# Memory numerators and denominators in one 136-column matmul per block, with the head gate folded into the memory matrix and new bias values for the scheduler

## The chip, the cores and the metric

The kernel runs on one core of a Trainium2 chip. The metric is the device time of one execution in microseconds. A run that is read closely comes with a profile of one execution. The profile's own span is about 1.7 us shorter than the time of the same run (268.6 us in the profile against 270.2 us timed, for the kernel before), so I compare spans with spans and times with times.

The engines are called PE (TensorE matmul), PEld (its weight loads), DVE (VectorE), ACT (ScalarE), POOL (GpSimd) and SP (SyncE, which issues most loads here). "PE idle" means that neither a matmul nor a weight load starts. One more number: the granted clock of PE. Most executions show 1.0, some 0.994 or less. For one core the program names as slow only runs more than 1.5% above the fastest of the same kernel, so runs with a clock of 0.994 may be labelled fast.

## The reference, cut to what matters

```python
# x: 2048 tokens, 512 wide; 32 heads of 16; 4 segments of 512 tokens
for s in range(4):
    qs, ks, vs = q[s], k[s], v[s]
    a_dot = softmax(qs @ ks.T * 0.25 + causal_mask) @ vs       # attention in the segment
    pq    = phi(qs)                                            # t>0: t+1, else exp(t)
    num   = pq @ M                                             # per head: 16 x 16 memory
    den   = pq @ z + 1e-6                                      # per head: 16-vector
    o     = g * num / den + (1 - g) * a_dot                    # g = sigmoid(beta), per head
    M    += phi(ks).T @ vs ;  z += phi(ks).sum(0)
a = concat(o) @ wo
b = (gelu(x @ w_gate) * (x @ w_up)) @ w_down                   # feed-forward, 512 -> 1792 -> 512
out = G * a + (1 - G) * b                                      # G = sigmoid(x . gate_w), per token
```

Segment 0 has no memory yet, so the memory part (num, den) runs three times, for segments 1, 2 and 3. The kernel computes it while PE works on the attention of the segment before.

## The kernel before: the parts that the argument touches

The program is a graph of tasks. A list scheduler places the tasks on the engines at build time, using estimated durations and a priority for each task. The priority is the longest estimated path below the task plus a bias value by the task's name. The result is one fixed order of instructions per engine. Loads are tasks of SP in the same graph.

```python
class Task:
    def __init__(self, name, alts, grp=None, after=(), bias=0.0, nbytes=0):
        self.bias = bias + BIAS.get(name[:re.search(r"[_.]|$", name).start()], 0.0)
...
        for t in reversed(topo):
            best = max([s.prio for s in t.succs] + [0.0])
            t.prio = min(t.est.values()) + best + t.bias
```

Attention of one row of heads: PE fills four score banks (`qk`), ACT takes the exp of all four at once (2048 columns), POOL masks, PE multiplies by the values (`pv`). There is only one set of score banks, so a fill waits for the exp of the fill before. In the gaps PE works on projections and the feed-forward, which rotate through four other banks (`psW`).

```python
prev_exp[0] = exp_task(s, f"exp{s}_{t}{name}", [Instr(lambda e: e.activation(
    dst[:], XALL[:, :].rearrange("p (g c) -> p g c", g=4), ACTF.Exp, scale=ATT_SCALE),
    [("X", g) for g in range(4)], [key], act_t(2048))], after=after)
```

The memory part, once per segment: 16 matmuls of 8 columns for the denominators, one DVE chain over them, then four groups of four matmuls of 128 columns for the numerators, each group evicted by one DVE multiply.

```python
pieces(f"den{s}", gd, [mm(gd, lambda qt=qt, t=t: gd.f32()[:, 32 * qt + 8 * t:32 * qt + 8 * t + 8],
                          phq[:, t, qt * 128:(qt + 1) * 128], MZbd[:, t, 16:136:17],
                          [("phq", t), ("MZbd", t)], True, True, 8)
                       for qt in range(4) for t in range(4)], 16)
task(f"denp{s}", DVE, [ ... add EPS, reciprocal (128 columns), multiply by Gm = G/(1-G) * g ... ])
for qt in range(4):
    pieces(f"num{s}_{qt}", gn, [mm(... 128 columns of MZbd[:, t, :] ...) for t in range(4)], 4)
    task(f"nump{s}_{qt}", DVE, [ ... otok = numerators * ndsc ... ], grp=gn)
```

The softmax here doesn't subtract the row's maximum and nothing guards it: scores larger than these inputs give would overflow.

Of the kernel before, what the change touches and what calls it, by code (L numbers as in the profile page):

```python
# [7 lines left out]
PE, ACT, DVE, POOL, SP = "pe", "act", "dve", "pool", "sp"  # L8
ENGINES = (PE, ACT, DVE, POOL, SP)

BF = mybir.dt.bfloat16
F32 = mybir.dt.float32
# [4 lines left out]
H = 32  # L17
# [18 lines left out]
    "D0": -106, "D1": -371, "D2": -43, "G0": -115, "G1": -247, "G2": -35, "G3": -378, "GdT0": 15, "GdT1": -60,  # L36
    "GdT2": 3, "GdT3": 30, "Gev0": 33, "K0": 3, "K1": -10, "K2": -10, "K3": -1, "Q0": 511, "Q1": -156, "Q2":
    -52, "Q3": -9, "U0": -34, "U1": 29, "U2": -14, "U3": -56, "Um0": 79, "Um1": 211, "Um2": 371, "V0": -1,
    "V2": 35, "Vev0": -104, "Vev1": 13, "Vev2": -60, "Vev3": -8, "Vlo0": -17, "Vlo2": -45, "den1": -2, "den2":
    -79, "den3": -12, "denp1": 8, "denp2": 6, "denp3": -190, "exp0": -301, "exp1": 30, "exp2": 6, "exp3":  # L40
    -129, "exsT0": 21, "exsT1": -14, "exsT2": 18, "exsT3": 15, "fin1": 4, "fin2": -31, "fin3": 65, "gate1":
    -309, "gate2": 79, "gate3": 2, "gelu0": 59, "gelu1": 464, "gelu2": -99, "gelu3": 47, "gexs0": -8, "gexs1":
    89, "gexs2": -293, "gexs3": 30, "gts0": -81, "gts1": -16, "gts2": 38, "gts3": -58, "kl0": -6, "kl1": 87,
    "kl2": 6, "kl3": -10, "kp0": -27, "kp1": 26, "kp2": 4, "kp3": 7, "msk1": -15, "msk2": 6, "msk3": 331,
    "mz0": 13, "mz1": 73, "mz2": 71, "mzacc0": -41, "mzacc1": -32, "mzacc2": -48, "mzbd0": -4, "mzbd2": 15,
    "norm1": -39, "norm2": 27, "norm3": -67, "num1": -760, "num2": -501, "num3": -80, "nump1": 383, "nump2":
    100, "nump3": 303, "oTd1": -9, "oTd2": -167, "oTd3": 66, "omg": 37, "pkT0": 62, "pkT2": 20, "pkc0": -46,
    "pkc2": -100, "pke0": 8, "pke2": 96, "pqc1": 89, "pqc2": -47, "pqc3": 27, "pqe1": 414, "pqe2": 41, "pqe3":
    1, "pv0": 210, "pv1": -139, "pv2": 95, "pv3": 98, "pvt0": 307, "pvt1": -156, "pvt2": 59, "pvt3": -4,
    "qk0": 13, "qk1": -19, "qk2": 49, "qk3": -61, "x2": 45, "x3": 76  # L50
# [301 lines left out]
def dve_t(n, mode=1, psum=False, ap=False):  # L352
    return max(0.19, 0.155 + n / mode / 960.0 + (0.06 if ap else 0.0))
# [11 lines left out]
def _build(es, nc, A_x, A_wq, A_wk, A_wv, A_wo, A_beta, B_w_gate, B_w_up, B_w_down, gate_w, out):  # L365
    def sb(name, shape, dtype=BF):
        return es.enter_context(nc.sbuf_tensor(name, shape, dtype))
# [24 lines left out]
    bdmask = sb("bdmask", [P, 2, 17])  # L392
    gatew = sb("gatew", [P, 4])
# [5 lines left out]
    exs = sb("exs", [P, 16], F32)  # L399
    stmp = sb("stmp", [P, 16], F32)  # L400
# [4 lines left out]
    Gm = [sb(f"gm{i}", [P, 4, H], F32) for i in range(2)]  # L405
    ndsc = sb("ndsc", [P, 4, H], F32)
# [28 lines left out]
    def task(name, eng, instrs, **kw):  # L435
        return S.add(Task(name, {eng: instrs}, **kw))
# [5 lines left out]
    def pieces(name, g, instrs, size, after=(), bias=0.0):  # L442

        r = None
        for i in range(0, len(instrs), size):
            r = task(f"{name}.{i}", PE, instrs[i:i + size], grp=g, after=after, bias=bias)
        return r
# [36 lines left out]
    def xdma(s, after=()):  # L484
        for kb in range(4):
# [10 lines left out]
    warm = PT[R_PT - 1][:, 0, :]  # L496
    wkey = ("PT", R_PT - 1)
# [5 lines left out]
    task("warm0", DVE, [Instr(lambda e: e.memset(warm[:, 0:128], 0.0), writes=[wkey], est=0.15)], bias=9999.0)  # L503
    task("tload", ACT, [Instr(lambda e: e.activation(stmp[:, 0:1], warm[:, 0:1], ACTF.Exp), reads=[wkey],
                              writes=[("stmp",)], est=1.5)], bias=8000.0)
# [15 lines left out]
    for i in range(7):  # L521
        gw = Grp(banks)
        n = 4 if i < 6 else 2
        task(f"warm{i}", PE, [Instr(lambda e, gw=gw, n=n: e.matmul(  # L524
            gw.f32()[:, 0:128 * n].rearrange("p (o c) -> p o c", c=128), warm[:, 0:128],
            warm[:, 0:128].rearrange("p (o c) -> p o c", o=1).to_broadcast([P, n, 128]), start=True, stop=True),
            [wkey], [gw.key], 0.107 * n)], grp=gw, bias=5000.0 - i)
# [50 lines left out]
    def gate_head():  # L578
        exp_task(0, "gexp", [Instr(lambda e: e.activation(gexp[:], betab[:], ACTF.Exp), [("w", "beta")],
                                   [("c", "gexp")], 0.25)])  # L580
        task("gmat", DVE, [
            Instr(lambda e: e.tensor_scalar(gtmp[:], gexp[:], 1.0, None, ALU.add), [("c", "gexp")],
                  [("c", "gtmp")], 0.2),
            Instr(lambda e: e.reciprocal(gtmp[:], gtmp[:]), [("c", "gtmp")], [("c", "gtmp")], 0.25),
            Instr(lambda e: e.tensor_tensor(gmat[:], gexp[:], gtmp[:], ALU.mult), [("c", "gexp"), ("c", "gtmp")],
                  [("c", "gmat")], 0.2)])
        omg = task("omg", POOL, [Instr(lambda e, g=g: e.tensor_copy(
            omgT[32 * g:32 * g + 32, :].rearrange("p (t j) -> p t j", j=2),
            gtmp[32 * g:32 * g + 32, :].rearrange("p (t g j) -> p g t j", g=4, j=2)[:, g]),
            [("c", "gtmp")], [("c", "omgT", g)], 0.3) for g in range(4)])  # L590
        for ins in omg.alts[POOL]:
            ins.fence = True
# [48 lines left out]
    def prep(s):  # L641
# [29 lines left out]
        for j in range(2):  # L671
# [10 lines left out]
        bc = lambda a: a.rearrange("p (a o) -> p a o", o=1).to_broadcast([P, 4, H])  # L682
        bh = lambda a: a.rearrange("p (o h) -> p o h", o=1).to_broadcast([P, 4, H])
# [4 lines left out]
            + ([Instr(lambda e: e.tensor_tensor(Gm[sl][:], bc(exs[:, s4]), bh(gmat[:]), ALU.mult),  # L688
                      [("exs", s), ("c", "gmat")], [("Gm", sl)], 0.3)] if s > 0 else []))
# [10 lines left out]
        if s > 0:  # L700
            for i in range(2):
                phi_task("pq", s, ph, qT[sl], ("qT", sl), phq, "phq", i)
            gd = Grp(banks)
            pieces(f"den{s}", gd, [mm(gd, lambda qt=qt, t=t: gd.f32()[:, 32 * qt + 8 * t:32 * qt + 8 * t + 8],
                                      phq[:, t, qt * 128:(qt + 1) * 128], MZbd[:, t, 16:136:17],
                                      [("phq", t), ("MZbd", t)], True, True, 8)
                                   for qt in range(4) for t in range(4)], 16)
            nf = ndsc[:].rearrange("p a h -> p (a h)")
            task(f"denp{s}", DVE, [
                Instr(lambda e: e.tensor_scalar(nf, gd.f32()[:, 0:128], EPS, None, ALU.add), [gd.key], [("nd",)],  # L710
                      0.3),
                Instr(lambda e: e.reciprocal(nf, nf), [("nd",)], [("nd",)], 0.95),
                Instr(lambda e: e.tensor_tensor(ndsc[:], ndsc[:], Gm[sl][:], ALU.mult), [("nd",), ("Gm", sl)],
                      [("nd",)], 0.3)], grp=gd)
            for qt in range(4):
                gn = Grp(banks)
                pieces(f"num{s}_{qt}", gn, [
                    mm(gn, lambda gn=gn, t=t: gn.f32()[:, 128 * t:128 * t + 128].rearrange("p (h e) -> p h e", e=16),
                       phq[:, t, qt * 128:(qt + 1) * 128],
                       MZbd[:, t, :].rearrange("p (h c) -> p h c", c=17)[:, :, 0:16],  # L720
                       [("phq", t), ("MZbd", t)], True, True, 128) for t in range(4)], 4)
                task(f"nump{s}_{qt}", DVE, [
                    Instr(lambda e, gn=gn, qt=qt: e.tensor_tensor(
                        otok[:, qt % 2, :].rearrange("p (h e) -> p h e", e=16),
                        gn.f32()[:, :].rearrange("p (h e) -> p h e", e=16),
                        ndsc[:, qt, :].rearrange("p (h o) -> p h o", o=1).to_broadcast([P, H, 16]), ALU.mult),
                        [gn.key, ("nd",)], [("otok", qt % 2)], dve_t(512))], grp=gn)
                dma(f"oTd{s}_{qt}", SP, lambda qt=qt: oT[sl][:, :, qt * 128:(qt + 1) * 128],
                    lambda qt=qt: otok[:, qt % 2, :], [("otok", qt % 2)], [("oT", sl, qt, t) for t in range(4)], 262144,
                    issue=1.25, transpose=True)  # L730

    def memory(s):
        sl = s % 2
        if s < NSEG - 1:
# [18 lines left out]
            else:  # L753
# [6 lines left out]
                bdmask[32 * c:32 * c + 32].rearrange("p (o j) e -> p o (j e)", o=1).to_broadcast([32, 4, 34]),  # L760
                ALU.mult), [("MZacc",)] + [("c", "bd", j) for j in range(2)], [("MZbd", t) for t in range(4)], 0.3)
# [339 lines left out]
```

## Time and profile before

| | before |
|---|---|
| time | 270.2 us (270.0 to 270.5, 4 runs) |
| span in the profile | 268.6 us |
| PE / ACT / DVE / POOL busy | 97% / 79% / 69% / 35% |
| first projection starts | 5.51 us |
| start-to-start steps of the 96 memory matmuls, as recorded | 3.70 + 1.83 us |

A start-to-start step is the time from the start of one matmul to the start of the next one on PE. I work with these because busy times of pipelined matmuls overlap and can't be added.

The page of the kernel before: busy time with share and instruction count, then the chain of work that ended last, by engine and by line.

```profile
PE 259.8 (97%) x3075; PEld 122.3 (46%) x3118; DVE 185.8 (69%) x333; ACT 211.9 (79%) x179; POOL 95.2 (35%) x223
...
PE 95%; issue 2%; ACT 2%; DVE 0%; ACTq 0%
```

The list of waits of the same kernel (us in total, times, longest):

```profile
ACT pt L782 <- PE psXALL L775: 24.3, 44, 1.0
PEld psXALL L775 <- ACT pt L782: 22.9, 54, 0.4
...
PE psW L524 <- DVE pt L503: 1.1, 1, 1.1
```

In the list of waits the matmul row of PE waits only at the warm-up. But for the weight loads of the score fills the list names ACT's exp in 54 of 72 fills. The length of these waits says nothing: the weight loads stand 0.42 us before all 69 fills that have such a wait, and in 10 of the 54 the exp had ended more than 0.2 us earlier. The line only points at the right place. The timeline decides: of the 68 fills that follow an exp of the same stretch, 50 start within 0.2 us of its end (0.055 us at the least), and 18 come 0.28 to 1.2 us after it. So PE comes to most fills just when the exp ends. In turn ACT waits for the fill. The two form a loop, and PE's other work has been cut to its length.

The groups of the memory part before (line, engine, operation, tiles, shapes, count, then busy us, mean ns of one, and idle time before them):

```profile
L723 DVE TENSOR_TENSOR otok<-psW,ndsc 128x512 bf16<-128x512 f32 x12 | 7.8, 681 | 7.9 <-PE psW L439 7.9
...
L439 PE MATMUL psW<-mzbd,phq 128*128 128x128 bf16 x48 | 4.2, 223 | 0.0
...
L712 DVE RECIPROCAL ndsc<-ndsc 128x128 f32<-128x128 f32 x3 | 2.9, 952 | 0.1
...
L439 PE MATMUL psW<-mzbd,phq 128*128 128x8 bf16 x48 | 1.7, 176 | 0.0
```

Finally one turn of the loop in the timeline of the kernel before, with the 16 denominator matmuls in it (start us, duration us, then as above):

```profile
46.53 0.41 PE L775 MATMUL psXALL<-qT,klow 32*128 32x64 bf16 x32
...
47.13 1.88 ACT L782 ACTIVATE ptl<-psXALL 128x2048 bf16<-128x2048 f32 x1 [0.16 <-PE psXALL L775]
...
47.32 0.58 PE L439 MATMUL psW<-mzbd,phq 128*128 128x8 bf16 x16
...
47.96 1.24 PE L439 MATMUL psW<-xT,wk 128*128 128x512 bf16 x5
...
49.13 0.12 PEld L775 LDWEIGHTS psXALL<-qT,kpad 32*128 32x128 bf16 x8 [0.42 <-ACT ptl L782]
...
49.73 1.88 ACT L782 ACTIVATE pt<-psXALL 128x2048 bf16<-128x2048 f32 x1 [0.23 <-PE psXALL L775]
```

### The profile page before, as it was taken

How to read it: one execution, taken by the hardware profiler on the slowest of the kernel's cores; microseconds unless marked ns; L12 is line 12 of the kernel's file. 1: busy time of each engine (PE TensorE's matmuls, PEld its weight loads, DVE VectorE, ACT ScalarE, POOL GpSimd, SP SyncE). 2: the span in 40 equal slices, each digit the busy share in tenths (PEclk: the TensorE clock that was granted, in tenths of full speed). 3: DMA queues.
4: the chain of work that ended last, by engine and by line, in shares of the span. 5: the costliest groups of instructions: out<-in, count | busy, mean ns of one | idle time of the engine just before them, and what ended most of it. 6: DMA issues, size and time to landing. Idle time of an engine off the chain costs nothing.

```text
span 268.6 us, 7243 instructions
## 1 busy us (share of the span) xinstructions
PE 259.8 (97%) x3075; PEld 122.3 (46%) x3118; DVE 185.8 (69%) x333; ACT 211.9 (79%) x179; POOL 95.2 (35%) x223
## 2 busy tenths in 40 slices
PE   8999999999999999999999999999999999999996
PEld 5445344444445444544444444444354434444354
DVE  1678997988978659798525988798851677353451
ACT  3889987999998898889768898877777767677602
POOL 8328853542002843252201574252300252352300
PEclk9999999999999999999999999999999999999999
DMA  6998991000304510102011310213020000000002
GB/s 194 203 323 185 362 212 22 4 0 2 81 2 98 81 42 0 45 20 42 20 24 39 60 23 1 58 27 82 1 44 0 2 0 2 20 22 32 9 2 78
DMA packets 32056, 16.53 MB, mean 62 GB/s; under 512 B 21400, under 2 KB 32024, under 8 KB 32024
## 3 DMA queue, kind: packets, MB, share of 16 engines
q1 hardware_dynamic: 31736, 15.81, 25.4%
q8 instruction: 24, 0.39, 0.6%
q10 hardware_dynamic: 288, 0.26, 0.3%
q14 instruction: 8, 0.07, 0.1%
HBM read 8.14 MB, written 2.10 MB: 38 GB/s over the span
## 4 chain that ended last, share of the span: by engine, by line
PE 95%; issue 2%; ACT 2%; DVE 0%; ACTq 0%
PE psW L439 75%; PE psXALL L775 9%; PE psW L824 6%; PE psXALL L439 1%; PE psW L832 1%; PE psW L524 1%; PE psW L742 1%; ACT pt L782 1%; PE psXALL L533 1%; ACT hT L909 1%; ACT L909 0%; ACT ost L958 0%; DVE pt L503 0%; ACTq L336 0%
## 5 line engine op out<-in xcount | busy, mean ns | idle before, releaser
L782 ACT ACTIVATE pt<-psXALL 128x2048 bf16<-128x2048 f32 x64 | 120.0, 1875 | 27.4 <-PE psXALL L775 24.3
L786 POOL TENSOR_SCALAR_AFFINE_SELECT pt<-pt 128x256 bf16<-128x256 bf16 x128 | 55.4, 434 | 139.3 <-ACT pt L782 132.7
L439 PE MATMUL psW<-xT,wu 128*128 128x512 bf16 x214 | 51.0, 379 | 1.1 <-issue 0.8
L439 PE MATMUL psW<-xT,wg 128*128 128x512 bf16 x213 | 50.3, 380 | 1.4 <-issue 1.1
L439 PE MATMUL psW<-wd,hT 128*128 128x512 bf16 x201 | 49.9, 380 | 1.1 <-issue 1.0
L930 DVE TENSOR_TENSOR hT<-psW,hT 128x512 bf16<-128x512 f32 x56 | 37.5, 685 | 15.6 <-PE psW L439 15.4
L839 DVE STREAM_TRANSPOSE tb<-psW 128x512 f32<-128x512 f32 x32 | 21.1, 696 | 18.9 <-PE psW L832 18.8
L439 PEld LDWEIGHTS psW<-xT,wu 128*128 128x128 bf16 x224 | 20.6, 98 | 24.8 <-issue 1.7
L439 PEld LDWEIGHTS psW<-xT,wg 128*128 128x128 bf16 x224 | 20.3, 98 | 24.5 <-issue 1.7
L439 PEld LDWEIGHTS psW<-wd,hT 128*128 128x128 bf16 x210 | 18.8, 98 | 22.7 <-issue 2.7
L775 PE MATMUL psXALL<-qT,kpad 32*128 32x320 bf16 (+3 forms) x512 | 25.4, 273 | 0.0
L909 ACT ACTIVATE hT<-psW 128x512 bf16<-128x512 f32 x28 | 16.4, 597 | 7.5 <-PE psW L439 7.5
L786 POOL TENSOR_SCALAR_AFFINE_SELECT ptl<-ptl 128x2048 bf16<-128x2048 bf16 x8 | 17.1, 2138 | 8.7 <-ACT ptl L782 8.4
L775 PEld LDWEIGHTS psXALL<-qT,kpad 32*128 32x128 bf16 x512 | 7.6, 92 | 26.5 <-ACT pt L782 20.8
L824 PE MATMUL psW<-pt,vaug 128*17 128x192 bf16 (+3 forms) x512 | 18.9, 273 | 0.0
L782 ACT ACTIVATE ptl<-psXALL 128x2048 bf16<-128x2048 f32 x8 | 15.0, 1876 | 2.8 <-PE psXALL L775 2.7
L439 PE MATMUL psW<-xT,wk 128*128 128x512 bf16 (+1 forms) x66 | 15.8, 381 | 0.2 <-issue 0.2
L691 POOL COPY exsT<-exs 32x4 f32<-32x4 f32 x64 | 14.6, 228 | 3.7
L439 PE MATMUL psW<-wo,oT 128*128 128x512 bf16 x55 | 14.8, 380 | 0.7 <-issue 0.5
L439 PE MATMUL psW<-xT,wq 128*128 128x512 bf16 x60 | 14.9, 380 | 0.5 <-issue 0.3
L456 DVE CAST hT<-psW 128x512 bf16<-128x512 f32 x21 | 14.0, 679 | 1.7 <-PE psW L439 1.5
L439 PE MATMUL psW<-wv,xT 128*128 128x512 bf16 x62 | 15.1, 380 | 0.1
(94 smaller groups left out, 285.5 us busy)
## 6 DMA issues: line engine op xcount, KB each, us to landing
out_dram<-ost SPq DMA_DIRECT2D x15, 128.0 KB, 1.7
wg<-in_B_w_gate_dram SPq DMA_DIRECT2D x2, 896.0 KB, 6.4
wu<-in_B_w_up_dram SPq DMA_DIRECT2D x2, 896.0 KB, 6.8
wd<-in_B_w_down_dram SPq DMA_DIRECT2D x1, 1792.0 KB, 13.1
vlow<-vaug SPq DMA_DIRECT2D x8, 136.0 KB, 3.5
wv<-in_A_wv_dram SPq DMA_DIRECT2D x1, 512.0 KB, 6.2
wo<-in_A_wo_dram SPq DMA_DIRECT2D x1, 512.0 KB, 14.0
wk<-in_A_wk_dram SPq DMA_DIRECT2D x1, 384.0 KB, 4.8
```

Of the source, the lines that this page charges most:

```text
L439: return Instr(lambda e: e.matmul(view(), lhsT, rhs, start=first, stop=last), reads=reads, writes=[fkey if fkey is not None else g.key], e ...
L456: alts[DVE] = [Instr(lambda e: e.tensor_copy(dst(), src()), reads=reads, writes=writes, est=dve_t(n))]
L524: task(f"warm{i}", PE, [Instr(lambda e, gw=gw, n=n: e.matmul(gw.f32()[:, 0:128 * n].rearrange("p (o c) -> p o c", c=128), warm[:, 0:128], ...
L533: task(f"x0t{i}_{u}", PE, [Instr(lambda e, k=k, a=a, u=u, i=i, src=src: e.transpose(src[:, k, a * 128:(a + 1) * 128], xin[:, 2 * u + a, (2 ...
L691: cross = task(f"exsT{s}", POOL, [Instr(lambda e, g=g, c=c: e.tensor_copy(exsT[sl][32 * g:32 * g + 32, c:16:4], exs[32 * c:32 * c + 32, s4 ...
L775: instrs.append(Instr(lambda e, g=g, lhs=lhs, rhs=rhs, c0=c0, ncol=ncol: e.matmul(X[g][:, c0:c0 + ncol], lhs(32 * g), rhs(32 * g), start=T ...
L782: prev_exp[0] = exp_task(s, f"exp{s}_{t}{name}", [Instr(lambda e: e.activation(dst[:], XALL[:, :].rearrange("p (g c) -> p g c", g=4), ACTF ...
L786: task(f"msk{s}_{t}{name}", POOL, [Instr(lambda e, view=view, pat=pat, base=base: e.affine_select(out=view, in_=view, compare_op=ALU.is_ge ...
L824: instrs.append(Instr(lambda e, t=t, q=q, kb=kb, slot=slot, c0=c0: e.matmul(gp.f32()[32 * q:32 * q + 17, 128 * kb + 64:512], Vaug[sl][:, k ...
L839: task(f"pvt{s}_{t}_{j}", DVE, [Instr(lambda e: e.transpose(Tb[:, j, :], gp.f32()[:, :]), [gp.key], [("Tb", j)], dve_t(512))], grp=gp)
L909: lambda e, g=g, ft=ft, s=s: e.activation(hT[s % 2][:, ft, :], g.f32()[:, :], ACTF.Gelu_apprx_tanh),
L930: task(f"Um{s}_{ft}", DVE, [Instr(lambda e, g=g, ft=ft: e.tensor_tensor(hT[sl][:, ft, :], g.f32()[:, :], hT[sl][:, ft, :], ALU.mult), [g.k ...
```

## The change

The intent is to save the denominator matmuls. The memory matrix `MZbd` holds, for each head, 16 columns of M and one of z, so one matmul of 136 columns gives numerators and denominators together. 136 columns fit three times into a bank of 512, so groups of four become groups of three or two, 18 in place of 12 in all. The head gate g is multiplied into M once (`gbd`), so that only the token's gate is left for the denominator chain. The denominator columns of each group (24 or 16) are then handled in a short DVE chain of its own, six per segment. Further, the PE warm-up reads a constant instead of a tile that DVE clears first. And nearly all bias values are new, so the order of everything is.

```diff
 BIAS = {
-    "D0": -106, "D1": -371, "D2": -43, "G0": -115, ...        # 125 values, most under 100
+    "D0": -883, "D1": -881, "D2": -595, "D3": -474, ...       # 164 values, up to 900
 }
+        gb = task("gbd", POOL, [ gbd = gmat * bdmask, 8 pieces, and a copy for the z columns ])
-    MZbd = MZacc * bdmask
+    MZbd = MZacc * gbd
-            pieces(f"den{s}", ...16 matmuls of 8 columns...) ; task(f"denp{s}", ...)
-            for qt in range(4):
-                pieces(f"num{s}_{qt}", ...4 matmuls of 128 columns...) ; task(f"nump{s}_{qt}", ...)
+            for pr in range(2):
+                for k in range(3):
+                    blocks = [(2 * pr + k, t) for t in range(3)] if k < 2 else [(2 * pr, 3), (2 * pr + 1, 3)]
+                    pieces(f"num{s}_{pr}{k}", gn, [
+                        mm(gn, lambda gn=gn, i=i: gn.f32()[:, 136 * i:136 * i + 136],
+                           phq[:, t, qt * 128:(qt + 1) * 128], MZbd[:, t, :],
+                           [("phq", t), ("MZbd", t)], True, True, 136) for i, (qt, t) in enumerate(blocks)], 3)
+                    task(f"nump{s}_{pr}{k}", DVE, [ (den + EPS) * exr, reciprocal, multiply ], grp=gn)
-    task("warm0", DVE, [memset]) ... warm-up matmuls read it
+    ones = nc.const_aps.tensor(1.0, (P, 512), BF) ... warm-up matmuls read that
```

## The prediction

> **What bounds the kernel now.** TensorE. The page shows PE busy 97% (259.8 of 268.6 us); the chain that ended last is 95% PE; the granted clock is full; the list of waits has nearly nothing that PE waited for (1.1 us at the warm-up, then 0.2). ScalarE is at 79%, VectorE 69%, GpSimd 35%. Busy time of pipelined matmuls overstates, so I went by start-to-start steps in the trace: full 512-column matmuls follow at 216 ns, and what is lost is lost at changes of kind: score to full matmul 165 ns (57 times), full to score 96 (69), value to full 345 (15), memory to full about 145 (8: five at 221 to 240, three at 5). Outside that lie the head (first projection at 5.5 us) and the tail (2.7 us after the last matmul).
>
> **Removed.** 48 denominator matmuls of 8 columns with their weight loads. Their steps total 1.83 us (38 ns each with the leaving of the run; 27 ns within, the Trainium skill, "TensorE: Matmul & The Clock Gate", "Wait — 56ns, not 53.3ns?", gives a floor of about 25 ns, and the trace agrees). On VectorE, per segment: gate product 0.86, add 0.28, reciprocal 0.95, product 0.53, four evictions at 0.68 us: 16.0 us in all. Also the zero memset and the warm-up's wait for it.
>
> **Added.** 48 x 8 columns (0.16 us). Twelve groups of four become 18 of three: up to six more exits. VectorE: six chains per segment of add-scale, reciprocal, multiply, by similar ops about 1.1 us each (estimate), 20 us in all, so +4 us, off the chain. GpSimd: nine small ops once, about 2 us near 15 us. A segment uses six banks instead of five, each held longer (1.1 against 0.68 us).
>
> **Moved.** Nearly all bias values changed, so the static order of everything does. With PE never waiting, a new order can only save changes of kind (a score followed by a value matmul saves about 0.1 us; ten of 16 already are) and a little at head and tail: estimate 0 to 2 us.
>
> **On the critical path.** Memory matmuls cost 5.5 us of PE steps (3.70 + 1.83), plus 0.4 entering from score and value matmuls. After: 48 x about 62 ns = 3.0, plus exits of 18 groups, 0 to 2.3 us: 3.0 to 5.3. Saving 0.6 to 2.9, say 1.6 us. The order: 0.7. Earlier warm-up: 0.1. The work added to VectorE and GpSimd costs nothing as long as evictions keep ahead of four banks; VectorE is at 42 of 48 us between 20 and 68 us, so some may show as bank waits: +0.3.
>
> **Predicted: 268.0 us** (0.8% less), range 266.0 to 270.2. Chances: faster by over 2% 0.05, within 2% 0.93, slower by over 2% 0.02.
>
> **What would show it.** Steps of the memory matmuls sum to 3.0 to 5.3 us, no 8-column forms; PE still 97% busy and over 93% of the chain; VectorE busy about 190 us against 185.8; the first projection within 0.3 us of 5.5; the tail unchanged.
>
> **What would make it wrong.** The new order puts groups of three where they leave slowly, or VectorE queues evictions so that PE waits for banks: same or slower. Or the old order hid losses at score and value changes that the search for bias values found (over 3 us): near 265. Or the clock ramp at the head moves: 0.7 us either way.

## More of the kernel before

One caution that the prediction missed: some matmuls have no record (the page has 3118 weight loads and 3075 matmuls), and a step that spans a missing full matmul is 216 ns too long. Laid beside the weight loads, five such steps leave a memory matmul in this profile. Without them the sums are 3.06 + 1.40 us. They also explain the five exits of "221 to 240" ns in the prediction.

From exp to exp are 2.60 us: 1.88 us of exp, and the rest for the hand-over to PE, the fill and the hand-over back. The PE work between the fills just fits.

## The result and the profile after

| | before | after |
|---|---|---|
| time of fast runs | 270.02 to 270.46 us (4 runs) | 272.62, 272.70, 273.19 us |
| further run, slow, clock 0.994 | | 276.77 us |
| ratio of fast runs | | 1.0097 (1.0081 to 1.0113) |
| span in the profile | 268.6 us | 271.5 us |

Ratios here and below are the mean time of one kernel's fast runs over that of the other's of the same rounds, so they are not quite the ratio of the medians that I quote. The change made the kernel 1% slower (the interval of the ratio is clear of 1); I had forecast 0.8% faster, and the measured time lies outside my range.

The page after, the same two lines:

```profile
PE 258.6 (95%) x3029; PEld 120.1 (44%) x3070; DVE 189.3 (70%) x370; ACT 212.8 (78%) x180; POOL 99.3 (37%) x232
...
PE 86%; DVE 5%; ACT 3%; issue 3%; DMA 2%; SPq 0%; ACTq 0%
```

PE is busy 1.2 us less, and the span is 2.9 us longer. DVE and a load appear in the chain. The memory part after, from the groups:

```profile
L446 PE MATMUL psW<-mzbd,phq 128*128 128x136 bf16 x48 | 5.5, 224 | 0.0
...
L733 DVE RECIPROCAL ndsc<-ndsc 128x24 f32<-128x24 f32 x12 | 3.6, 303 | 0.4
```

The 8-column matmuls are gone. In start-to-start steps as recorded the memory matmuls went from 3.70 + 1.83 us to 4.26 us. What PE loses on entering them from score or value matmuls went from 0.39 to 0.85 us, so the part as a whole fell from 5.9 to 5.1 us: 0.8 us less. Here too five of the steps span a missing full matmul (3070 weight loads, 3029 matmuls). Without them 4.8 us fell to 4.0 us, and the difference is the same.

Where did the time go? I cut both spans at the start of the first exp of each segment:

| stretch (first exp to first exp) | before | after | difference |
|---|---|---|---|
| start to segment 1 | 80.64 us | 83.61 us | +2.97 |
| segment 1 to segment 2 | 64.09 | 63.97 | -0.12 |
| segment 2 to segment 3 | 63.22 | 63.26 | +0.04 |
| segment 3 to the end | 60.67 | 60.64 | -0.03 |

The whole loss lies in the first 84 us. From there on the stretches differ by 0.12 us at most, although one of the three memory parts lies in each of the first three stretches. So there are two questions: what costs 3 us in the first stretch, and why does the cheaper memory part show nowhere else?

For the first question, the list of waits after has these entries of PE, which the list before does not have:

```profile
PEld psW L852 <- issue: 2.0, 1, 2.0
PE psW L446 <- DMA wk<-in_A_wk_dram: 1.8, 1, 1.8
PE psW L844 <- issue: 1.8, 1, 1.8
...
PE psW L446 <- DVE hT L463: 0.9, 1, 0.9
```

The first and the third are one stall. The three stalls in order of time:

**Head.** The first projection starts at 6.86 us instead of 5.51 (timeline before, then after):

```profile
5.51 4.33 PE L439 MATMUL psW<-xT,wk 128*128 128x256 bf16 x20
...
6.86 2.75 PE L446 MATMUL psW<-xT,wk 128*128 128x512 bf16 x12 [1.80 <-DMA wk<-in_A_wk_dram]
```

It waits for wk. In the new order SP issues the last 384 columns of wk first (issued 1.74 us, landed 6.72), and PE starts with tiles that read them. Before, the first 128 columns came first (issued 1.75 us, landed 5.20). This pair overstates the difference: in the six profiles with the old load order in this document the start lies between 5.51 and 6.48 us (mean 5.87), and in five of the new order with its head unedited between 6.03 and 6.86 (mean 6.52). The loads land at different times from one execution to the next: the first part of wk between 5.12 and 6.34 us in those six.

**33 us.** PE stops in the middle of a value matmul task. Timeline after:

```profile
32.71 0.61 PE L844 MATMUL psW<-pt,vaug 128*17 128x448 bf16 x15
...
35.09 0.19 PE L844 MATMUL psW<-pt,vaug 128*17 128x64 bf16 x1 [1.78 <-issue]
35.09 0.17 PEld L852 LDWEIGHTS psW<-ptl,vlow 128*17 128x17 bf16 x16 [1.96 <-issue]
```

"issue" means that the profile shows nothing that PE waited for. The weight load at 35.09 does carry a semaphore, that of the second vlow load, but this load had landed at 25.28 us.

**52 us.** PE waits for a bank that DVE evicts late:

```profile
49.50 2.12 POOL L806 TENSOR_SCALAR_AFFINE_SELECT ptl<-ptl 128x2048 bf16<-128x2048 bf16 x1 [1.63 <-ACT ptl L802]
49.59 2.56 DVE L875 TENSOR_TENSOR obf<-tb,sc 128x512 bf16<-128x512 f32 x1
...
52.82 1.85 DVE L463 CAST hT<-psW 128x512 bf16<-128x512 f32 x3
...
53.53 0.82 PE L446 MATMUL psW<-xT,wg 128*128 128x512 bf16 x3 [0.86 <-DVE hT L463]
```

The DVE multiply took 2.56 us; the median of its group is 0.74. It began 0.09 us after a POOL mask of 2.12 us. The Trainium skill, "SBUF — State Buffer", section "Who interferes with whom", says that a DVE instruction with two SBUF inputs and a GpSimd instruction that reads SBUF exclude each other, for the whole of the one that began first. The trace agrees: the multiply ended at 52.15 us, 0.53 us after the mask (by itself it takes a little longer than that, 0.74). The kernel before has five DVE instructions that run 0.3 to 1.9 us long beside a mask as well (three of them with two inputs in SBUF), but at places where no bank ran out.

The three stalls add up to 4.2 us (1.35, 1.97 and 0.91), more than the 3.0 that were lost, so the new order must be better elsewhere in this stretch.

### The profile page after: what moved, and what is told of

Same layout as the page of the kernel before. It is cut to its first block, busy times and chain, and to the rows that moved or that the text cites. A ratio compares the mean times of both kernels' runs of the same rounds, so it can differ in the third digit from the quotient of the medians.

```text
span 271.5 us, 7190 instructions
## 1 busy us (share of the span) xinstructions
PE 258.6 (95%) x3029; PEld 120.1 (44%) x3070; DVE 189.3 (70%) x370; ACT 212.8 (78%) x180; POOL 99.3 (37%) x232
## 4 chain that ended last, share of the span: by engine, by line
PE 86%; DVE 5%; ACT 3%; issue 3%; DMA 2%; SPq 0%; ACTq 0%
PE psW L446 70%; PE psXALL L795 8%; PE psW L844 5%; DMA wk<-in_A_wk_dram 2%; PE psXALL L446 1%; ACT pt L802 1%; DVE hT L463 1%; ACT hT L929 1%; PE psW L852 1%; ACT L929 1%; DVE gmat L589 1%; DVE qT L463 1%; DVE hT L950 0%; PE psW L761 0%; SPq L477 0%
## 5 line engine op out<-in xcount | busy, mean ns | idle before, releaser
L806 POOL TENSOR_SCALAR_AFFINE_SELECT pt<-pt 128x256 bf16<-128x256 bf16 x128 | 56.0, 439 | 137.8 <-ACT pt L802 128.3
L446 PE MATMUL psW<-xT,wu 128*128 128x512 bf16 x214 | 51.8, 379 | 1.2 <-issue 1.0
L446 PE MATMUL psW<-xT,wq 128*128 128x512 bf16 x61 | 15.5, 380 | 0.2
L446 PE MATMUL psW<-wv,xT 128*128 128x512 bf16 x62 | 14.4, 379 | 0.2 <-DVE ndsc L733 0.2
L875 DVE TENSOR_TENSOR obf<-tb,sc 128x512 bf16<-128x512 f32 x16 | 13.8, 864 | 0.5
```

Of the source, the lines that this page charges most:

```text
L446: return Instr(lambda e: e.matmul(view(), lhsT, rhs, start=first, stop=last), reads=reads, writes=[fkey if fkey is not None else g.key], e ...
L806: task(f"msk{s}_{t}{name}", POOL, [Instr(lambda e, view=view, pat=pat, base=base: e.affine_select(out=view, in_=view, compare_op=ALU.is_ge ...
L875: Instr(lambda e: e.tensor_tensor(ov, tv[:, :, :, 0:16], rb, ALU.mult), [("Tb", 0), ("Tb", 1), ("sc1", i2)], [("obf",)], 0.79),
```

## The experiments

Most experiments leave the order that the scheduler made as it is and move single tasks in it afterwards, before the instructions are emitted:

```python
order = list(S.schedule())
def move(names, after): ...      # takes tasks out of the order and puts them behind another one
```

In this way one suspected cause is changed and the other engines keep their instruction streams, which I compared. Dependencies are planned from the order after the move. The runs of one job share a chip and the runs of the kernel before on it; I name the jobs A to D. The kernel before had a median of 270.38 us in A (11 runs), 270.63 in B (11), 270.53 in C (9) and 270.41 in D (11).

### The stall at 33 us (job A)

My theory was that PE had run out of instructions. The packet records of the trace show 24 fetches of 16,384 bytes on a queue of their own, labelled as instructions. Together they are 393,216 bytes, 63.9 for each of the 6,154 recorded PE instructions, so these are PE's, in blocks of about 256. The rival was the vlow load, whose semaphore the stalled instruction carries.

**Big weights later.** Only SP's order changes.

```diff
+    move(["w_wo", "w_('wu', 1)", "w_('wu', 0)", "w_wd"], after="x2_3")
```

> The changed kernel with the four big weight loads (wo, wu twice, wd; 4.1 MB) issued after the four transposing loads of x instead of before them; PE, VectorE, ScalarE and GpSimd orders untouched. Theory A (the 1.96 us stall inside the value matmuls at 33 us is PE waiting for its own next 16 KB of instructions, whose fetch sits behind the weight burst on the DMA engines): the fetch that lies at 32.6 us comes within about 2 us of 29.3 us, the stall disappears, time falls by 1.5 to 2.0 us. Theory B (PE waits there for the load of vlow, the semaphore named on the stalled instruction): nothing changes, since vlow is issued before the weights in both: within 0.3 us.

Measured: 271.10 us median of 6 runs, ratio to before 1.0034 (1.0008 to 1.0060). The stall is gone; timeline of this run at the same place:

```profile
32.45 0.61 PE L844 MATMUL psW<-pt,vaug 128*17 128x448 bf16 x16
...
32.86 0.19 PEld L852 LDWEIGHTS psW<-ptl,vlow 128*17 128x17 bf16 x16
```

**vlow first.**

```diff
+    move(["Vlo0_1"], after="Vlo0_0")
```

> The changed kernel with the second vlow load issued right after the first, one transposing load earlier; nothing else moved. Theory A (instruction fetch behind the weight burst): the stall at 33 us stays at about 1.9 us and the time within 0.3 us. Theory B (the wait is for vlow): vlow lands about 1.3 us earlier, the stall shrinks by that or vanishes, time falls by 1.3 to 1.9 us.

Measured: the stall stays, and is 2.24 us long. The rival falls. The time was 275.16 us (4 runs, all with a clock of 0.994 or less), so slower than the first measurement of the changed kernel. This missed my expectation, and the profile tells why. Windows of this run (us, then busy time of PE, PEld, DVE, ACT and POOL with counts, the granted clock, DMA share, GB/s):

```profile
30.00:32.00 2.00, 1.84 (x16) 0.75 (x16) 1.53 (x6) 1.93 (x2) 1.61 (x7) 1.00 1.05 381
35.10:38.40 3.30, 2.76 (x29) 0.95 (x30) 2.11 (x5) 0.71 (x2) 2.29 (x8) 0.50 1.13 342
40.00:43.00 3.00, 3.00 (x21) 1.10 (x19) 2.32 (x5) 2.56 (x4) 1.37 (x2) 1.00 1.41 136
```

At the end of the stall PE's clock fell to half, by the record from 35.08 to 38.49 us, and ACT waited with it: it was busy for 0.71 of the 3.30 us in the second window, and for 2.11 in the same window of the first profile, at full clock. The first window also shows what the fetch had to pass: 381 GB/s of weights.

**Forty useless matmuls.** Work is added, nothing is moved.

```diff
+    named["K0_1.0"].alts[PE] = [40 matmuls of one column into its bank] + named["K0_1.0"].alts[PE]
```

> The changed kernel with 40 useless one-column matmuls (80 PE instructions) ahead of the first projection, where PE stands idle for wk anyway; every other instruction and every load as it was. They move PE's 256-instruction blocks by 80 instructions, so that the dense stretch of 64 memory-update and 64 value matmuls no longer falls into one block. Theory A: the block that begins at 29.2 us begins at about 24 us instead, its follow-up is fetched in time, the stall at 33 us disappears: 1.5 to 2.0 us faster although work was added. Theory B (vlow, or anything that waits for data): no change, or up to 1 us slower by the added matmuls.

Measured: 271.80 us, ratio 1.0059 (1.0032 to 1.0086), 6 runs. The stall is gone. No load or other engine's stream was changed here, so data are an unlikely cause. The size fell short of what I expected (1.5 to 2.0 us): against the full-clock runs of the changed kernel it is about 1 us, and the first projection started later, at 7.55 us.

The record of the fetches fits in all kernels. "Block" is the 256 recorded PE instructions before the one at which PE stopped, number 701:

| kernel | block begins | fetch: start, took | block done | PE then |
|---|---|---|---|---|
| before | 25.76 us | 29.39, 1.16 us | 34.58 us | goes on |
| after | 29.35 | 32.61, 1.13 | 33.12 | idle 1.97 us |
| vlow first | 29.29 | 32.67, 1.13 | 33.07 | idle 2.24 us |
| big weights later | 29.08 | 29.41, 1.30 | 32.86 | goes on |
| forty matmuls | 23.71 | 24.99, 0.95 | 32.83 | goes on |

In these records PE fetches the next block 0.3 to 3.6 us after it has begun one, and the short delays are those without the weight burst. Behind the weight burst the fetch came 3.3 to 3.6 us late, in the kernel before as well. There the block lasted 8.8 us, so nothing was seen. In the changed order 64 memory-update matmuls and two value tasks fell into one block, which lasted only 3.8 us. The Trainium skill, "Runtime: NRT & Kernel Launch", section "Instruction fetch mechanics", gives blocks of 16 KiB (256 instructions), fetched while the current one runs, and calls the cost mostly hidden. The blocks agree; the hiding failed here by 2 us. One thing stays open: PE went on 1.35 us after the last packet of the fetch (33.74 to 35.09), and no record shows what that time is. In the other five profiles of the changed order with this stall it is 1.43 to 1.64 us.

### The head (jobs A and B)

**wk in two parts, first try.**

```diff
-    wk columns 128 to 512 in one load
+    wk columns 128 to 256, then wk columns 256 to 512
```

> The changed kernel with one load cut in two: the first 128 columns of wk that the first projection reads come by themselves (128 KB) ahead of the next 256, all engines' orders otherwise as they are. Theory (the new bias values put a 384 KB load first, and PE stood 1.97 us for it): the first projection starts at about 5.5 us instead of 6.86, and the time falls by 0.6 to 1.4 us (PE's clock may still be at half until about 6.9 us, then it is nearer 0.6). Rival (the head is hidden, since later stages wait for ScalarE and DMA anyway): the start moves and the time stays within 0.3 us. The stalls at 33 and 52 us stay.

Measured: 275.97 us (5 of 6 runs with a clock of 0.994 or less), slower. This run failed as a test: I had named the dependency of the first part with the key 1, which Python takes to be equal to True, the key of the second. So the second load was issued only when the first had landed, at 5.42 us, and the first projection started at 8.53 us (the next expectation says 8.47). It shows the other direction, a head that starts 1.7 us later, but together with the clock.

**wk in two parts, mended.**

> The wk load cut in two as in the first try, mended: there the two halves shared a key by mistake, so that the second waited for the first to land and the first projection started at 8.47 us. Now both are issued back to back. Theory (the order of the first loads costs the head): wk's first 128 columns land at about 5.3 us, the first projection starts at 5.4 to 5.7 us instead of 6.86, time 0.6 to 1.4 us under the unedited changed kernel. Rival (head hidden): within 0.3 us of it. The stalls at 33 us (1.96 us) and 52 us (0.91 us) stay.

**The changed kernel again**, as the base of job B.

> The changed kernel once more, unedited, as the base of the experiments that run on the same chip with it. From the first pair: 0.8 to 1.1% slower than before when the clock record shows full speed all along (about 272.7 us), and some runs 2 to 4 us longer, with a mean clock of 0.994 or less, where the stall at 33 us is followed by a stretch of 3.4 us at half clock (as the profile of the run with vlow first shows).

Measured: the base had three runs with full clock, 272.68 to 272.96 us, and three with 0.994 or 0.988, 274.44 to 276.66 us. The mended split had six runs, all with full clock, 272.60 to 273.34 us, median 272.73. Its first projection started at 5.85 us. In this job the base itself started at 6.30 us, earlier than in the first profile. Runs of full clock differ by no more than the noise, so as a mend by itself the split did not show in the time, and my 0.6 us were not met. The stall at 33 us follows in both (2.02 and 2.05 us in the profiles), and part of the earlier start was lost again at once, since the next tile's part of wk and then gwrow were awaited. So for the head alone nothing is shown by this run. It is settled only together with the rest, below.

### The stall at 52 us (job B)

```diff
+    move(["norm0_1"], after="Gev1_3")        # on DVE: four evictions, then the normalise task
```

> The changed kernel with one VectorE task (normalise, second value tile of the first row of heads) moved behind the three evictions that followed it; nothing else moved. Theory (its multiply of two SBUF operands, 2.56 us instead of 0.74, is locked out by GpSimd's 2.1 us mask that started 0.09 us before it, and PE then waits 0.91 us for a bank): the 0.91 us PE stall at 52 us goes, the multiply takes under 1.1 us, time falls by 0.6 to 0.9 us. Rival (PE would have been held there by ScalarE's next exp anyway): the stall goes and the time stays within 0.3 us.

Measured: the 0.91 us stall is gone, and the multiply takes 0.69 us. But a stall of 0.68 us came up 4 us later (below), and five of six runs had a clock of 0.994 (the profile of one of them shows the half-clock stretch after 33 us). The median is 274.50 us; the one run with full clock took 272.59. By its time alone this run is inconclusive.

### All mends together (jobs B and C)

**First mended kernel:** wk in two parts, big weights later, the normalise task later.

> The three mends together on the changed kernel: wk cut in two, big weights after the loads of x, the normalise task behind the evictions. If the three stalls explain the loss and the cheaper memory matmuls are worth the 0.8 to 1.3 us that their steps show, the time is 0.3 to 1.3 us under the kernel before (269.0 to 270.0 us where before is 270.3) and 3 to 4.5 us under the unedited changed kernel. If something else of the new order costs, it stays over the kernel before.

Measured: 270.57 us (270.38 to 271.10, 6 runs, all with full clock); ratio to before 0.9997 (0.9972 to 1.0023). The loss (2.2 us in this job, full-clock runs against the kernel before) is gone, so the stalls explain it, but the gain that I had still counted on is missing. The profile shows two remaining waits: 0.53 us at the head for the last part of wk, and 0.66 us at 53 us. There PE waits for a bank whose memory numerators DVE evicts late, since I had put the normalise task directly ahead of them:

```profile
54.00 0.90 PE L446 MATMUL psW<-xT,wq 128*128 128x512 bf16 x3 [0.66 <-DVE otok L741]
```

**Second mended kernel:**

```diff
+    move(["w_wv"], after="w_('wq', True)")
-    move(["norm0_1"], after="Gev1_3")
+    move(["norm0_1"], after="Gev1_4")
```

> The changed kernel with all mends, two of them wider than in the first mended one: wv loaded after wk and wq (PE stood 0.53 us for the last part of wk), and the normalise task behind one more eviction and the memory numerators (which held a bank that PE wanted for 0.68 us). Everything else as in the changed kernel. Theory: both stalls go, 0.8 to 1.3 us under the first mended kernel (270.57 us): 269.2 to 269.8 us, which is 0.3 to 0.5% under the kernel before and shows what the memory matmuls are worth. Rival (a new order only shifts the waits): 270.3 us or more.

Measured: 269.75 us (269.61 to 269.85, 5 runs, clock 0.999 or 1.0), ratio to before 0.9971 (0.9959 to 0.9984). This is faster than the kernel before by 0.3% and than the changed kernel by about 3 us, and its result is correct. The page:

```profile
PE 259.0 (97%) x3029; PEld 120.4 (45%) x3070; DVE 186.9 (70%) x370; ACT 212.6 (79%) x180; POOL 101.0 (38%) x232
```

Its four stretches are 80.14, 63.98, 63.26 and 60.62 us. Against the changed kernel the first fell by 3.47 us, the others by nothing. Nearly all of its lead over the kernel before (0.6 us of span) lies in the first stretch too.

### The parts exchanged (job C)

The obvious way to separate order and structure is to give each kernel the other's bias values.

> The changed code with the bias values of before: the structure alone, if the two parts were separable. Bias values steer a list scheduler for one graph of tasks, so I expect that the old ones fit the new graph worse than either pair fits: 272 to 280 us, with new waits of PE at places where neither kernel has them. If instead only the new values are to blame, it is 268.5 to 270 us.

> The code of before with the new bias values: the order alone, if separable. It should have the late first projection (wk's 384 KB part first, start at 6 to 7 us instead of 5.5) since the load order follows from the bias values, and further waits of its own as the values were made for another graph: 272 to 280 us. If the memory change itself were the cause of the loss, this would be at 270.3 us or under.

Measured: the changed code with the old values took 277.51 us (ratio 1.0273), the old code with the new values 284.44 us (1.0449; its four runs have clocks from 0.976 to 0.993). Both are much slower than either kernel. In the second the first projection waits 2.5 us at the head, and a value task stands for 4.1 us at 35 us. That is the stall at 33 us again, in other code: PE stood ahead of its 703rd record, and the fetch of that block began at 36.92 us, took 1.15, and PE went on at 39.30. The values belong to their graph: exchanged, they make new waits of their own, and these two runs say little about the two parts by themselves. That is why the moves above were needed.

### Where the gain went (jobs C and D)

**Denominators cut.** On the kernel before, with all orders kept.

```diff
-    16 denominator matmuls of 8 columns per segment
+    one matmul of 128 columns into the same bank
```

> The kernel before, all orders as they are, with the 16 denominator matmuls of each segment replaced by one of 128 columns (the result is wrong on purpose: the denominators are no longer those of the heads). It measures by itself what the removal is worth where PE bounds. Their steps sum to 1.83 us; three matmuls of 128 columns and the leaving of three runs remain, 0.3 to 0.7 us. Theory (PE steps count one for one): 1.1 to 1.5 us faster than before, about 269.0 us. Rival (VectorE, ScalarE or the banks bound those stretches): within 0.4 us of before, with the freed time found as new waits of PE.

Measured: 270.22 us against 270.53; ratio 0.9991 (0.9977 to 1.0005). Once more in job D:

> The denominator cut once more, as the base of the next run on this chip (wrong result on purpose): 0.1 to 0.5 us faster than before, as the first time.

Measured: 270.63 us against 270.41; ratio 1.0010 (0.9988 to 1.0033). So 1.1 us of PE work were taken out (1.29 us of denominator steps in the fully recorded profile of the control below, less 0.18 us for the three matmuls put in), and the time did not move beyond noise. The timeline of the second run shows where they went:

```profile
47.46 1.88 ACT L782 ACTIVATE ptl<-psXALL 128x2048 bf16<-128x2048 f32 x1 [0.16 <-PE psXALL L775]
...
47.65 0.22 PE L439 MATMUL psW<-mzbd,phq 128*128 128x128 bf16 x1
...
49.39 0.12 PEld L775 LDWEIGHTS psXALL<-qT,kpad 32*128 32x128 bf16 x8 [0.72 <-ACT ptl L782]
49.39 0.40 PE L775 MATMUL psXALL<-qT,kpad 32*128 32x448 bf16 x8 [0.23 <-ACT ptl L782]
```

The weight load now stands for 0.72 us and no longer for the usual 0.42, and the matmul row shows 0.23 us of open idle time: PE now comes too early and waits for the exp.

**Denominators twice.** The opposite edit on the kernel before, with the result unchanged.

> The kernel before with the 16 denominator matmuls of each segment done twice (same result), all orders kept: 0.43 us of PE work added at three places. Theory (steps are the longer of PE work and the exp loop, and both are equal there): adding costs in full though removing gained nothing: 1.0 to 1.4 us slower than before. Rival (idle PE time there): within 0.3 us.

Measured: 272.12 us, ratio 1.0062 (1.0044 to 1.0079), 6 runs. That is 1.7 us, more than the 1.3 us added; the profile has a second wait of 0.68 us for wk at the head, at 7.49 us, so part of it is not the edit's. Timeline at the same place:

```profile
47.72 1.00 PE L439 MATMUL psW<-mzbd,phq 128*128 128x8 bf16 x32
...
49.96 0.12 PEld L775 LDWEIGHTS psXALL<-qT,kpad 32*128 32x128 bf16 x8 [0.42 <-issue]
```

Now the fill waits for nothing but PE. The step from exp start to exp start, at the three places where denominators lie:

| | segment 1's | segment 2's | segment 3's |
|---|---|---|---|
| cut (second run) | 2.52 us | 2.53 us | 2.52 us |
| before | 2.60 | 2.53 | 2.59 |
| twice | 3.02 | 2.93 | 3.02 |

Taking 0.4 us out of a step shortened it by 0 to 0.08 us, and adding 0.43 us lengthened it by 0.40 to 0.43. A step is as long as the longer of two things: the PE work put into it, and the loop of fill, exp and hand-overs, which takes about 2.52 us here. At these places the tuned order had made them nearly equal. That rules out idle PE time there as well as a pure PE bound.

**Cut, and filled up.** From each cut to the end of its stretch, every fill goes behind one more pair of full matmuls (25 moves; PE's order alone changes).

> The denominator cut, and from each cut to the end of its attention stretch every score fill moved behind one more pair of full matmuls in PE's order (25 moves), so that 0.43 us of later work fills each freed place; the other engines' orders as before. Wrong result on purpose, as in the cut. Theory: the freed time is collected at the end of each stretch: 0.5 to 1.1 us faster than the plain cut, 0.8 to 1.4 us faster than before. Rival: no more than 0.2 us faster than the plain cut.

**The same moves without the cut**, as the control.

> The control: the same 25 moves in the kernel before with its denominators kept (result unchanged). The work is only dealt differently over steps that are all full: the first step of each stretch grows by 0.43 us and the PE-only stretch after it shrinks by that. Theory: within 0.3 us of before. If this alone is 0.5 us or more faster, the gain of the run above comes from the move and not from the cut.

Measured: cut and filled 270.93 us, ratio 1.0015 (1.0001 to 1.0029), 5 runs; filled alone 272.19 us, ratio 1.0063 (1.0049 to 1.0077), 6 runs. Both expectations were missed in one way: the moves cost about 1.8 us by themselves, since at three places (132, 182 and 198 us) PE now starts nothing for 0.5, 0.9 and 0.4 us, at value matmuls and behind memory matmuls. But between the two runs, which differ by the cut alone, the cut is worth 1.26 us (272.19 less 270.93), all of the 1.1 us of PE work within the noise. The stretches of the profiles say the same without the head, which varies: the second and third are 0.36 and 0.35 us shorter with the cut than without it, where in the tuned order the cut took 0.00 and 0.05 to 0.07 us off them. By time the same cut was worth 0.3 us and nothing there, in two tries. So what saved PE time is worth depends on whether the order has work to put into its place.

## Why the prediction was wrong, point by point

- **"What bounds the kernel now. TensorE."** This step failed first. It holds for the stretches between the attention stretches, but not inside them. There a step is the longer of PE's work and the exp loop, and in 50 of 68 steps PE came within 0.2 us of the exp's end. I took 97% busy and an empty matmul row in the list of waits for a PE bound. The hint against it was in the same list, under the weight loads (ACT named in 54 of 72 fills). The Trainium skill, "Trainium Kernel Development and Optimization", section "Performance Expectations", warns that matmul busy time is a bad metric for how close a kernel is to roofline. This fits the warning: the kernel before was 97% busy, and cutting 1.1 us of PE work from it moved the time by 0.3 us at most.
- **"Saving 0.6 to 2.9, say 1.6 us."** The work did shrink, by 0.8 us of steps (5.9 to 5.1 as recorded, 4.8 to 4.0 without the missing records), inside my range but half of my middle value. As time it was hardly collected: the second and third stretches, with a memory part in each, changed by -0.12 and +0.04 us.
- **"With PE never waiting, a new order can only save changes of kind ... The order: 0.7."** This step had the wrong sign, and it is the larger error: I had counted on a gain of 0.7 us, and the new order cost 3 us in the first stretch. I thought of an order as something that could only make better use of PE. It also decides which load goes first, which DVE and POOL instructions collide, and which instructions share a 16 KB block when weights are being loaded. Mending exactly these took the changed kernel from 272.7 us or more to 270.57 and then to 269.75.
- **"VectorE ... some may show as bank waits: +0.3."** The mechanism was right and the size was too small: 0.91 us at one place, and that by a collision with POOL, not by the amount of DVE work. DVE's busy time of 189.3 us was as predicted ("about 190").
- **"The first projection within 0.3 us of 5.5; the tail unchanged."** The projection started at 6.86 us, because I did not follow the bias values to the loads (and because this start varies by itself, between 5.51 and 6.48 us with the old load order). The tail stayed (2.6 us after the last matmul, 2.7 before).
- **"PE still 97% busy and over 93% of the chain."** It was 95% and 86%.
- **"Or the clock ramp at the head moves: 0.7 us either way."** The clock did play a part, but later: in two profiles it falls to half for 3.4 us after the stall at 33 us, and the runs with a clock of 0.994 or less are about 2 to 4 us longer.
- **Open.** How much each of the three stalls costs by itself is shown for the stall at 33 us only (ratio 1.0034 with late weights against 1.0097 without, in different jobs). The head and the stall at 52 us are shown by the mended kernels together, not one by one. That saved PE time is lost to the exp loop was tested on the kernel before only; that it goes the same way in the changed order is argued from the equal stretches.

## What to carry to other kernels

A high busy share of PE is not a PE bound: look at what its weight loads wait for, and test a supposed saving by cutting the work out and by doubling it, since a step that is full on two sides answers differently to each. When a change comes with a new static order, read the new order before you cost the arithmetic: which load is first, what the first matmul needs, where two engines meet on SBUF. In a stretch of many small matmuls, remember that PE's own instructions come by DMA, behind whatever has been issued before.

## What the Trainium skill lacked or had wrong

- "Runtime: NRT & Kernel Launch", "Instruction fetch mechanics", gives PE 128 KiB of instruction memory in one sentence, and in another says of instruction memory in general that it is two lines of 16 KiB. Here PE stood still at its 701st recorded instruction while one block of 16 KB was late, which fits the two blocks. The page also says that the cost is mostly hidden. It was 1.97 to 2.24 us when the fetch met 381 GB/s of weight loads and the block of 256 instructions ran in 3.8 us.
- "TensorE: Matmul & The Clock Gate", "What's actually happening", lets the clock fall after an idle window of about 3.4 us. In two profiles a stall of 2.24 us was followed by half clock for 3.41 us; in four others stalls of 1.97, 2.02, 2.03 and 2.05 us were not. The length of the stall alone does not decide: in the changed code with the old values a stall of 1.62 us that ended at 172.08 us was followed by half clock from 173.35. Of 32 runs with the stall at 33 us, 18 had a clock of 0.994 or less (five of the 18 are runs of the failed wk split, whose head was late as well); of the 23 runs of changed kernels in which that stall was mended, two had, and of 42 runs of the kernel before in jobs A to D, none. What decides between them was not settled.
- No page that I read says that a PE stall of that kind appears as "issue" on an instruction whose semaphore was met long before (here 9.8 us: vlow landed at 25.28 us, PE went on at 35.09).
- "SBUF — State Buffer", "Who interferes with whom", was right: 2.56 us in place of 0.74 for a multiply that began 0.09 us after a mask of 2.12 us.
